# The 47-point products of four sequences, from float32 to one float32r product that carries a rest, with a sum made in DRAM

## Chip, core and metric

The kernel runs on one core of a Trainium2 chip. A core has five engines that run their own queues in order and meet through semaphores: TensorE (PE, matrix products into PSUM), VectorE (DVE), ScalarE (ACT), GpSimd (POOL) and SyncE (SP). SP issues most transfers; POOL issues some, and those that add to what stands at their destination. The metric is the device time of one execution in microseconds (us); less is better. Before the change it is 2776.86 us (median of three runs, 2776.58 to 2780.26).

## What is computed

```python
# x: (8, 3008, 256)
X = rfft(x, axis=1)                                  # along the sequence
Yr = Xr @ w_r - Xi @ w_i + b_r
Yi = Xr @ w_i + Xi @ w_r + b_i
Y  = sign(Y) * max(abs(Y) - 0.01, 0)                 # real and imaginary part apart
y  = irfft(Yr + 1j * Yi, n=3008, axis=1)
t  = y.reshape(24064, 256)
out = (sigmoid(t @ w_gate) * (t @ w_val)) @ w_out    # 1536 hidden columns
```

The inputs are float32, the weights of the last line float64.

## The kernel before

The transform over 3008 = 47 x 64 points is done in two steps. The step that the change touches is the first, "a": for each of the 64 residues, a 47-point real transform, that is a product with a matrix of 47 rows and 48 columns (24 frequencies, real and imaginary). `fa` holds this matrix twice, once for each of two interleaved halves j of the residues, so that one float32 product of 94 rows, 96 output rows and 512 columns (two residues of 256 channels) does both halves. One step `(b, h)` of sequence b covers eight residues: a load `load_a` of 384 KB into a tile `xf` (L181), two products `pa` (L186), two copies from PSUM back into `xf` (L187) and a store `store_a` into the DRAM array `zd` of that sequence (L197). The copies are ACT's, save for one of two in the first two sequences.

The second step reads `zd` back frequency by frequency (`load_b`, tile `zf`, L239), does a 64-point product (`fwd_b`, tile `pb`, L247), mixes channels (`mix`, `pm`, L282), thresholds, and goes back (`inv_b`, `pi`, L319 to L321, then `inv_a`, `pia`, L351). These products, except L247 and L351, are float32r: a value is split into a rounded part and a rest, and the product is the sum of three.

The eight sequences stand in groups of 1, 1, 2, 2 and 2. The dense part (`ffn1`, products `pg` and `pv` at L410 to L412, and `ffn2`, `po` at L438 to L440) of the first nine chunks of tokens runs unit by unit from `ffn`, 108 units in all, and between these units stands the "side" work: the transforms of the later groups. The last two groups' steps "a" are the lists `a3` and `a4`, 16 steps each. Each side piece has a weight (`1.7` for a step "a"), and a piece is issued when enough weight has come together (`rates`, `acc`). From there on the order on each engine is set by a scheduler that works at build time; the earlier part is written out by hand under `manual_schedule`. After the ninth chunk the rest of the dense part runs alone, to the end.

PSUM has eight banks: three for transforms (tag `fft`, so `pa`, `pb`, `pm`, `pi` and `pia` take turns), three for `pg` and `pv`, two for `po`. A bank is free again when ACT or DVE has read it. The tiles of step "a" come from five buffers of 4 KB a partition with the tag `big`; raw weights and, later, `make_t` (POOL's combining of weights, L535 to L551) take buffers of the same tag.

```python
        def step_a(i):
            if i == 0:
                for k in range(min(PRE, len(aa))):
                    load_a(*aa[k])
            if i + PRE < len(aa):
                load_a(*aa[i + PRE])
            fwd_a(*aa[i])
            store_a(*aa[i])
```

Of the kernel before, what the change touches and what calls it, by code (L numbers as in the profile page):

```python
# [9 lines left out]
F32 = mybir.dt.float32  # L10
F32R = mybir.dt.float32r
# [3 lines left out]
ALU = mybir.AluOpType  # L15
# [4 lines left out]
R2, R1 = 47, 64  # L20
NK2 = 24
NQ = 2 * NK2
# [4 lines left out]
HW = 512  # L27
FFT_BANKS, L1_BANKS, L2_BANKS = 3, 3, 2

NF2K, NR2K, NLD, NST, NBIG, NMF, NME, NVF, NVO, NHH, NSG, NYF = 5, 4, 3, 3, 5, 3, 2, 3, 1, 3, 2, 3  # L30
NCB, NTMP, NHP = 10, 9, 12


# [1 line left out]
PRE = 2  # L35
# [13 lines left out]
def _split(v):  # L49
    hi = _r12(v)  # L50
    lo = _r12(v - hi)
    return hi.astype(np.float32), lo.astype(np.float32)
# [13 lines left out]
def _tables(seq):  # L66
    n2 = np.arange(R2)
    k2 = np.arange(NK2)
    c, s = _cs(n2[:, None] * k2[None, :], R2)
    fa = np.zeros((R2, 2, NK2, 2, 2))  # L70
    fb = np.zeros((NK2, 2, 2, 128))
    for j in range(2):
        fa[:, j, :, 0, j] = c
        fa[:, j, :, 1, j] = -s
        fb[:, 0, j, j:2 * R2:2] = c.T / seq
        fb[:, 1, j, j:2 * R2:2] = -s.T / seq
    fa = fa.reshape(2 * R2, 2 * NQ)
    fb = fb.reshape(2 * NQ, 128).astype(np.float32)
    n1 = np.arange(R1)
    k1 = np.arange(R1)  # L80
    mf = np.zeros((NK2, 128, 128), np.float32)
    mi = np.zeros((NK2, 128, 128), np.float32)
    mis = np.zeros((NK2, 128, 2, 128), np.float32)
    for q in range(NK2):
        k = q + R2 * k1
        c, s = _cs(n1[:, None] * k[None, :], seq)
        flip = np.where(k > seq // 2, -1.0, 1.0)
        m = np.zeros((2, R1, 2, R1))
        m[0, :, 0] = c
        m[1, :, 0] = s  # L90
        m[0, :, 1] = -s * flip
        m[1, :, 1] = c * flip
        w = np.full(R1, 2.0)
        if q == 0:
            w[k > seq // 2] = 0.0
            w[(k == 0) | (2 * k == seq)] = 1.0
        e = np.zeros((2, R1, 2, R1))
        e[0, :, 0] = (w * c).T
        e[1, :, 0] = (-w * flip * s).T
        if q:  # L100
            e[0, :, 1] = (w * s).T
            e[1, :, 1] = (w * flip * c).T
        mf[q] = m.reshape(128, 128)
        mi[q] = e.reshape(128, 128)
        mis[q, :, 0], mis[q, :, 1] = _split(e.reshape(128, 128))
    return {"mf": mf, "mi": mi, "mis": mis, "fa": fa.astype(np.float32), "fb": fb}


@with_exitstack
def tile_fft_mix_ffn(ctx: ExitStack, tc, x, w_r, w_i, b_r, b_i, w_one, w_out, mf, mi, mis, fa, fb, out):  # L110
    nc = tc.nc

    B, D, S = x.shape[0], w_r.shape[0], R1 * R2
    P = 128
    XR = x.shape[2]
    CT = D // P
    NF = w_one.shape[0]
    NP = NK2 // 2
# [18 lines left out]
    cw = fft.enter_context(tc.tile_pool(name="cw", bufs=1))  # L137
    p2 = fft.enter_context(tc.tile_pool(name="p2", bufs=2))
# [4 lines left out]
    def bank(name, tag="fft", bufs=FFT_BANKS):  # L143
        return (psf if tag == "fft" else psl).tile([P, 512], F32, tag=tag, bufs=bufs, name=name)
# [5 lines left out]
        gap("gap_r", 320)  # L150
        return p2.tile([P, 2, D], F32R, tag="r2k", bufs=NR2K, name=name)

    fa_sb = cw.tile([2 * R2, P], F32, name="fa_sb")[:, :2 * NQ]
    nc.scalar.dma_start(fa_sb, fa)

    zd = [tc.dram_tile([NQ, R1, D], F32, name=f"zd{b}") for b in range(B)]
# [4 lines left out]
    xv = x.rearrange("b u p (h c) -> b u p h c", c=D)  # L161
# [3 lines left out]
    held = {}  # L165
# [10 lines left out]
    def big(name):  # L176
        return p2.tile([P, 4, D], F32, tag="big", bufs=NBIG, name=name)

    def load_a(b, h):
        xf = p0.tile([P, 4, D], F32, name="xf0", bufs=R1 // 8) if b == 0 else big("xf")  # L180
        nc.sync.dma_start(xf[:XR], xv[b, h])  # L181
        held["x", b, h] = xf

    def product_a(xi, az, copy):
# [4 lines left out]
    def fwd_a(b, h):  # L189

        xf = held["x", b, h]
        for i in range(2):
            at = slice(2 * i, 2 * i + 2)
            product_a(xf[:2 * R2, at], xf[:2 * NQ, at], nc.vector.tensor_copy if b < 2 and i else nc.scalar.copy)

    def store_a(b, h, queue=nc.sync):
        queue.dma_start(zv[b][:, 4 * h:4 * h + 4], held.pop(("x", b, h))[:2 * NQ])  # L197

    def load_half(b, h):
        xf = r2k("xfh").bitcast(F32)  # L200
        nc.sync.dma_start(xf[:XR], xv[b, h // 2, :, h % 2 * 2:h % 2 * 2 + 2])
        held["xh", b, h] = xf

    def half_a(b, h):
# [246 lines left out]
    def fft_units(bs, ms):  # L451


        aa = [(b, h) for b in bs for h in range(R1 // 8)]
        units = []

        def step_a(i):
            if i == 0:
                for k in range(min(PRE, len(aa))):
                    load_a(*aa[k])  # L460
            if i + PRE < len(aa):
                load_a(*aa[i + PRE])
            fwd_a(*aa[i])
            store_a(*aa[i])

        def loads(q, b):
            if b == bs[0]:
                if q == 0:
                    ms[0, 0] = load_mf(0)
                if q + 1 < NP:  # L470
                    ms[q + 1, 0] = load_mf(q + 1)
                if 0 <= q - 1 < NP and (q - 1, 1) not in ms:
                    ms[q - 1, 1] = load_mi(q - 1, False)
            if q == 0:
                load_b(b, 0)
            if q + 1 < NP:
                load_b(b, q + 1)

        def step(q, b):
            loads(q, b)  # L480
            if q < NP:
                fwd_b(b, q, ms[q, 0], False)
            if 0 <= q - 1 < NP:
                mix(b, q - 1)
            if 0 <= q - 2 < NP:
                inv_b(b, q - 2, ms[q - 2, 1], False)

        first = [(1.7, lambda i=i: step_a(i)) for i in range(len(aa))]
        for q in range(NP + 2):
            wt = 0.9 * (q < NP) + 2.0 * (0 <= q - 1 < NP) + 0.7 * (0 <= q - 2 < NP)  # L490
            units += [(wt, lambda q=q, b=b: step(q, b)) for b in bs]
        return first, units
# [259 lines left out]

    bias_sb = cw.tile([P, 2, D], F32, name="bias_sb")
    bias4 = p0.tile([P, D], F32, name="bias4")
    ebias = cw.tile([P, P], F32, name="ebias")[:, :1]
    fb_sb = const.tile([2 * NQ, P], F32, name="fb_sb")
    w1h = const.tile([P, NF, 2, CT, P], F32R, name="w1h")
    w1l = const.tile([P, NF, 2, CT, P], F32R, name="w1l")
# [182 lines left out]
    p0s.close()  # L941
    p3 = p3s.enter_context(tc.tile_pool(name="p3", bufs=2, side="right", reuse_waits="tile"))
    with tc.manual_schedule():
        for u in own0:
            load_v(u)
        load_part()
        halves(AT_FIRST)
        for f in range(NF):
            ffn[f]()
            if parts:  # L950
                load_part()
            if f in (2, 3):
                tables[f - 2, 1] = load_mi(f - 2, False, later=True)
            if f in (5, 6):
                keep_mi(f - 5, tables[f - 5, 1])
            halves(AT_FIRST + (f + 1) * (len(beside) - AT_FIRST) // NF)
# [44 lines left out]
    for j in range(NF, len(ffn)):  # L1001
        c, f = divmod(j, NF)
# [39 lines left out]
    a, b, c, d = banks[0]  # L1042
# [62 lines left out]
```

## Time and profile before

| what | value |
|---|---|
| median of three runs | 2776.86 us (2776.58 to 2780.26) |
| the profiled execution | 2779.58 us |
| its span in the trace | 2777.7 us |
| TensorE clock granted | 0.999 in the mean |
| instructions in the span | 38257 |
| HBM read, written | 134.17 MB, 104.33 MB |

A row of the groups gives the line of the kernel, the engine, the operation, the tile written and the tiles read, the shape, how often, the busy time and the mean duration, and then the time that the engine idled just ahead of these, with what ended it. A row of the stretches gives for each engine the busy time and number of instructions, then PE's granted clock, the mean busy share of the 16 DMA engines, and their rate. PE products overlap in the pipeline; one instruction of float32 appears as two records. PEld is the loading of weights into PE.

### The profile page before, as it was taken

Reading aid. Unit: us, or ns where it says so; the run is one execution under the profiler, and the core shown is the slowest. Engines: PE = TensorE matmul, PEld = TensorE weight load, DVE = VectorE, ACT = ScalarE, POOL = GpSimd, SP = SyncE. Lnnn points to the kernel's source line nnn. Section 1 sums busy time; section 2 is a strip of 40 time slices with the busy share of each in tenths; the row PEclk is TensorE's granted clock in tenths of the full one; section 3 lists DMA queues with packets and bytes.
Section 4 is the critical chain, followed back from the end, with each engine's and each line's share of the span. In section 5 each row is a group of like instructions: output and inputs, shape, how many; then the busy total and the mean of one; then the engine's idle time right before and its main releaser. Section 6 shows DMA issues by size and latency. Waiting matters only on the chain.

```text
span 2777.7 us, 38257 instructions
## 1 busy us (share of the span) xinstructions
PE 2760.4 (99%) x13896; PEld 2305.2 (83%) x13896; DVE 2080.6 (75%) x3109; ACT 1307.4 (47%) x2276; POOL 709.4 (26%) x638
## 2 busy tenths in 40 slices
PE   9999999999999999999999999999999999999999
PEld 6778888888899988888888888888888888888887
DVE  5778778767787636777777777777777777777776
ACT  4665554555455444444444444444444444444443
POOL 0211010223200001333333343333333333333321
PEclk9999999999999999999999999999999999999999
DMA  9867545665554561000000000000000000000000
GB/s 293 266 214 198 171 139 157 193 190 184 178 156 147 168 196 58 31 16 16 31 31 16 16 31 31 31 11 21 31 31 16 16 31 31 27 4 31 31 16 16
DMA packets 173469, 241.01 MB, mean 87 GB/s; under 512 B 14592, under 2 KB 124896, under 8 KB 173280
## 3 DMA queue, kind: packets, MB, share of 16 engines
q1 hardware_dynamic: 163776, 214.93, 25.0%
q0 software_dynamic: 9408, 23.60, 2.6%
q8 instruction: 110, 1.80, 0.3%
q14 instruction: 79, 0.65, 0.1%
q10 hardware_dynamic: 96, 0.04, 0.0%
HBM read 134.17 MB, written 104.33 MB: 86 GB/s over the span
## 4 chain that ended last, share of the span: by engine, by line
PE 95%; DVE 3%; DMA 1%; ACT 1%; issue 0%; SPq 0%; DVEq 0%; ACTq 0%
PE pd L670 11%; PE pc L670 11%; PE pa L670 11%; PE po L646 7%; PE po L645 7%; PE po L647 7%; PE pb L670 6%; PE pm L282 5%; PE pia L351 4%; PE pa L186 3%; PE pb L247 3%; PE pg L410 2%; PE pg L411 2%; PE pg L412 2%; PE pv L410 2%; PE pv L412 2%
## 5 line engine op out<-in xcount | busy, mean ns | idle before, releaser
L647 PE MATMUL po<-hl,w 128*128 128x512 f32 x912 | 354.8, 389 | 0.0
L645 PE MATMUL po<-hh,w 128*128 128x512 f32 x912 | 354.8, 389 | 0.0
L646 PE MATMUL po<-hh,w 128*128 128x512 f32 x912 | 354.8, 389 | 0.0
L729 POOL TENSOR_TENSOR c<-c,c 128x512 f32<-128x512 f32 x114 | 147.7, 1296 | 801.2 <-DVE c L725 588.1
L670 PE MATMUL pc<-s,w1h 128*128 128x512 f32 x912 | 280.8, 389 | 0.0
L670 PE MATMUL pa<-a,w1h 128*128 128x512 f32 x912 | 280.8, 389 | 0.0
L725 DVE TENSOR_TENSOR c<-u,pc 128x512 f32<-128x512 f32 x228 | 156.5, 687 | 91.5 <-PE pc L670 85.6
L700 DVE TENSOR_TENSOR u<-u,pb 128x512 f32<-128x512 f32 x228 | 155.2, 681 | 90.7 <-PE pb L670 61.1
L617 ACT CAST hh<-v 128x512 fp32r<-128x512 f32 x114 | 70.7, 620 | 306.1 <-DVE v L710 306.1
L645 PEld LDWEIGHTS po<-hh,w 128*128 128x128 f32 x912 | 171.2, 188 | 35.6
L670 PEld LDWEIGHTS pc<-s,w1h 128*128 128x128 f32 x912 | 171.2, 188 | 35.5
L670 PEld LDWEIGHTS pa<-a,w1h 128*128 128x128 f32 x912 | 171.2, 188 | 35.5
L647 PEld LDWEIGHTS po<-hl,w 128*128 128x128 f32 x912 | 171.2, 188 | 35.5
L646 PEld LDWEIGHTS po<-hh,w 128*128 128x128 f32 x912 | 171.2, 188 | 35.5
L621 POOL TENSOR_TENSOR hl<-c,hh 128x512 fp32r<-128x512 f32 x114 | 152.3, 1336 | 186.0 <-ACT hh L617 186.0
L282 PE MATMUL pm<-w_sb,xsh 128*128 128x256 f32 x1008 | 188.5, 286 | 1.6 <-ACT xf L187 1.1
L670 PE MATMUL pc<-s,w1l 128*128 128x512 f32 x456 | 177.4, 389 | 0.0
L670 PE MATMUL pa<-a,w1l 128*128 128x512 f32 x456 | 177.4, 389 | 0.0
L702 DVE TENSOR_TENSOR v<-u,pc 128x512 f32<-128x512 f32 x228 | 156.9, 688 | 24.5 <-DVE u L700 0.9
L731 DVE TENSOR_TENSOR u<-u,pd 128x512 f32<-128x512 f32 x228 | 156.6, 687 | 24.5 <-DVE c L725 0.9
L704 DVE TENSOR_TENSOR v<-v,pd 128x512 f32<-128x512 f32 x228 | 156.7, 687 | 24.0 <-DVE v L702 0.5
L696 ACT COPY u<-pa 128x512 f32<-128x512 f32 x228 | 133.7, 586 | 69.4 <-PE pa L670 69.2
(174 smaller groups left out, 6721.1 us busy)
## 6 DMA issues: line engine op xcount, KB each, us to landing
zf<-zd SPq DMA_DIRECT2D x96, 256.0 KB, 3.6
vf<-vd SPq DMA_DIRECT2D x128, 192.0 KB, 3.0
out_dram<-ot SPq DMA_DIRECT2D x93, 256.0 KB, 2.2
vd<-vz SPq DMA_DIRECT2D x84, 256.0 KB, 2.8
ypair<-yd SPq DMA_DIRECT2D x19, 1024.0 KB, 4.9
yd<-yf SPq DMA_DIRECT2D x103, 188.0 KB, 2.9
xf<-in_x_dram SPq DMA_DIRECT2D x48, 384.0 KB, 4.1
zd<-xf SPq DMA_DIRECT2D x44, 384.0 KB, 3.3
```

Source lines behind the costliest of these rows:

```text
L282: nc.tensor.matmul(o, l, r, start=(i == 0), stop=(i == len(mms) - 1))
L621: sub_(hl, h, hh)
L645: nc.tensor.matmul(o, wh, hh, start=(f == 0), stop=False)
L646: nc.tensor.matmul(o, wl, hh, start=False, stop=False)
L647: nc.tensor.matmul(o, wh, hl, start=False, stop=(f == NF - 1))
L670: nc.tensor.matmul(o, l, r, start=not more and l is wh and r is xh, stop=l is wl, skip_group_check=more)
L700: add(u, u, b)
L702: add(v, u, c)
L704: add(v, v, d)
L725: add(c12, u, c)
L729: nc.gpsimd.tensor_mul(c12, g12, c12)
L731: add(u, u, d)
```

## The change

For the steps of `a3` and `a4` only, the float32 product gives way to a float32r product. For each half j (47 rows, of which 64 are loaded; the 17 others meet rows of zeros in the matrix) the step

- loads 64 rows of x into a tile `aw` (SP, L205),
- writes the rounded x into rows 0 to 63 of a tile `xw` (ACT, L212) and minus the rounded x into rows 64 to 127 (ACT, L211),
- lets a transfer of POOL's queue read the same 64 rows of x again and add them to rows 64 to 127 (L213), which then hold the rest x minus its rounding,
- does two products of 128 rows, 128 output rows and 512 columns with the matrix `fw` (L223): its first 48 columns hold the rounded 47-point matrix for the rounded x and, in the lower rows, for the rest; its columns 64 to 111 hold the matrix's own rest for the rounded x,
- copies 112 rows of each result into `aw` (ACT, L224),
- stores rows 0 to 47 into `zd` (SP, L231) and, once that has landed, adds rows 64 to 111 to the same place (POOL's queue, L232).

So a step has four float32r products in place of two float32 ones, four copies in place of two, four splitting instructions, and two loads, two stores and four adding transfers in place of one load and one store. The `big` buffers grow from five to eight; the room comes from the scratch of POOL's transfers (4096 bytes a partition). The weight of a step falls from 1.7 to 0.95. The rows of x are laid out on the host with the halves one after the other, and padded to 112.

```diff
-NF2K, NR2K, NLD, NST, NBIG, NMF, NME, NVF, NVO, NHH, NSG, NYF = 5, 4, 3, 3, 5, 3, 2, 3, 1, 3, 2, 3
+NF2K, NR2K, NLD, NST, NBIG, NMF, NME, NVF, NVO, NHH, NSG, NYF = 5, 4, 3, 3, 8, 3, 2, 3, 1, 3, 2, 3
...
+    fw = np.zeros((128, 128), np.float32)
+    fw[:R2, :NQ], fw[:R2, 64:64 + NQ] = _split(fa[0, :, :, :, 0].reshape(R2, NQ))
+    fw[64:64 + R2, :NQ] = fw[:R2, :NQ]
...
+    def load_w(b, h):
+        for j in range(2):
+            at = xv[b, h, j * R2:j * R2 + 64]
+            r = p2.tile([P, 4, D], F32R, tag="big", bufs=NBIG, name="xw")
+            t = big('aw')
+            nc.sync.dma_start(t[:64], at)
+            held['w', b, h, j] = r, t
+
+    def split_w(b, h):
+        for j in range(2):
+            r, t = held["w", b, h, j]
+            nc.scalar.mul(r[64:], t[:64], -1.0)
+            nc.scalar.copy(r[:64], t[:64])
+            nc.gpsimd.dma_start(r[64:], xv[b, h, j * R2:j * R2 + 64], accum_op=ALU.add)
+
+    def fwd_w(b, h):
+        for j in range(2):
...
+            for i in range(2):
+                pa = bank("pw")
+                at = slice(2 * i, 2 * i + 2)
+                nc.tensor.matmul(pa, fw_sb, r[:, at], start=True, stop=True)
+                nc.scalar.copy(t[:64 + NQ, at], pa[:64 + NQ].rearrange("p (h c) -> p h c", h=2))
+            held["w", b, h, j] = t
+
+    def store_w(b, h):
+        for j in range(2):
+            t = held.pop(("w", b, h, j))
+            z = zd[b][:, j * R1 // 2 + 4 * h:j * R1 // 2 + 4 * h + 4]
+            nc.sync.dma_start(z, t[:NQ])
+            nc.gpsimd.dma_start(z, t[64:64 + NQ], accum_op=ALU.add)
...
         def step_a(i):
-            if i == 0:
-                for k in range(min(PRE, len(aa))):
-                    load_a(*aa[k])
-            if i + PRE < len(aa):
-                load_a(*aa[i + PRE])
-            fwd_a(*aa[i])
-            store_a(*aa[i])
+            for k in (0, 1) if i == 0 else (i + 1,):
+                if k < len(aa):
+                    load_w(*aa[k])
+                    split_w(*aa[k])
+            fwd_w(*aa[i])
+            store_w(*aa[i])
...
-        first = [(1.7, lambda i=i: step_a(i)) for i in range(len(aa))]
+        first = [(0.95, lambda i=i: step_a(i)) for i in range(len(aa))]
...
+        nc.gpsimd.dma_start(fw_sb, fw)
...
-    nc = _bacc.Bacc("TRN2", target_bir_lowering=False, num_devices=1)
+    nc = _bacc.Bacc("TRN2", target_bir_lowering=False, num_devices=1, dynamic_dma_scratch_size=4096)
...
-    x = given["x"].reshape(b, 2 * R2, R1 // 8, 4 * d).transpose(0, 2, 1, 3)
-    given["x"] = np.ascontiguousarray(np.pad(x, ((0, 0), (0, 0), (0, 2), (0, 0))))
+    x = given["x"].reshape(b, R2, 2, R1 // 8, 4 * d).transpose(0, 3, 2, 1, 4).reshape(b, R1 // 8, 2 * R2, 4 * d)
+    given["x"] = np.ascontiguousarray(np.pad(x, ((0, 0), (0, 0), (0, R2 + 64 - 2 * R2 + 1), (0, 0))))
```

How the scheduler places the new work is seen in three pieces of the built order. The lines of the changed file are 38 higher from L238 on (L410 becomes L448, L319 becomes L357). First PE, in a step of the group `a3`, before: the two float32 products stand together behind the `pi` products of a side unit and ahead of a dense unit's `pg`.

```order
L319 MATMUL pi_4227<-yh_4030,mi_sb_3899 128x256
L320 MATMUL pi_4227<-yl_4031,mi_sb_3899 128x256
L321 MATMUL pi_4227<-yh_4030,mi_sb_3899 128x256
L186 MATMUL pa_4239<-xf_3861,fa_sb_77 96x512
L186 MATMUL pa_4242<-xf_3861,fa_sb_77 96x512
L410 MATMUL pg_4246<-yth_1901,w1h_105 128x512
L411 MATMUL pg_4246<-ytl_1902,w1h_105 128x512
```

PE in a step of the same group, with the change: the four products of the two halves (`xw_4262` and `xw_4265`) are spread among the dense unit's products.

```order
L359 MATMUL pi_4437<-yh_4221,mi_sb_4117 128x256
L223 MATMUL pw_4459<-xw_4262,fw_sb_103 128x512
L448 MATMUL pg_4475<-yth_1902,w1h_105 128x512
L449 MATMUL pg_4475<-ytl_1903,w1h_105 128x512
L223 MATMUL pw_4462<-xw_4262,fw_sb_103 128x512
L450 MATMUL pg_4475<-yth_1902,w1l_106 128x512
L448 MATMUL pg_4475<-yth_1902,w1h_105 128x512
L223 MATMUL pw_4465<-xw_4265,fw_sb_103 128x512
```

The products that stood side by side now alternate with others, each with its own FFT bank.

Second ACT, behind those same four products: the four copies into `aw_4263` and `aw_4266`, one dense unit's sigmoid and cast, one transform unit's copies, and then the split of a later step, whose `xw_4649` lies in the buffer that `aw_4263` has had.

```order
L224 COPY aw_4263<-pw_4462 112x512
L331 CAST yh_4433<-yc_4430 128x512
L224 COPY aw_4266<-pw_4465 112x512
L224 COPY aw_4266<-pw_4468 112x512
L454 ACTIVATE sg_4489<-pg_4475 128x512
L464 CAST hh_4492<-sg_4489 128x512
L298 COPY xsf_4515<-pb_4508 128x2x2x2x64
L302 CAST xsh_4513<-xsf_4515 128x768
L361 COPY vz_4561<-pi_4554 128x512
L211 ACTIVATE xw_4649<-aw_4650 64x1024
L454 ACTIVATE sg_4578<-pg_4564 128x512
```

Before, this place on ACT held two copies L187 and nothing of the split.

Third POOL, whose queue had no transfer of step "a" in this group before. The adding stores of the step above stand ahead of the adding loads of the later one.

```order
L213 DMA xw_4447<-in_x_dram 64x1024
L213 DMA xw_4450<-in_x_dram 64x1024
L232 DMA zd5_86<-aw_4263 48x1024
L232 DMA zd5_86<-aw_4266 48x1024
L213 DMA xw_4649<-in_x_dram 64x1024
```

So the adding load into `xw_4649` is issued behind the adding store out of `aw_4263`.

More of the change, by code (lines that the diff above doesn't have):

```diff
@@ L69, in _tables @@
     c, s = _cs(n2[:, None] * k2[None, :], R2)
-    fa = np.zeros((R2, 2, NK2, 2, 2))
+    fa = np.zeros((2, R2, NK2, 2, 2))
     fb = np.zeros((NK2, 2, 2, 128))
     for j in range(2):
-        fa[:, j, :, 0, j] = c
-        fa[:, j, :, 1, j] = -s
+        fa[j, :, :, 0, j] = c
+        fa[j, :, :, 1, j] = -s
         fb[:, 0, j, j:2 * R2:2] = c.T / seq
         fb[:, 1, j, j:2 * R2:2] = -s.T / seq
+    fw = np.zeros((128, 128), np.float32)
+    fw[:R2, :NQ], fw[:R2, 64:64 + NQ] = _split(fa[0, :, :, :, 0].reshape(R2, NQ))
+    fw[64:64 + R2, :NQ] = fw[:R2, :NQ]
     fa = fa.reshape(2 * R2, 2 * NQ)
@@ L105, in _tables, with tile_fft_mix_ffn @@
         mis[q, :, 0], mis[q, :, 1] = _split(e.reshape(128, 128))
-    return {"mf": mf, "mi": mi, "mis": mis, "fa": fa.astype(np.float32), "fb": fb}
+    return {"mf": mf, "mi": mi, "mis": mis, "fa": fa.astype(np.float32), "fw": fw, "fb": fb}
 @with_exitstack
-def tile_fft_mix_ffn(ctx: ExitStack, tc, x, w_r, w_i, b_r, b_i, w_one, w_out, mf, mi, mis, fa, fb, out):
+def tile_fft_mix_ffn(ctx: ExitStack, tc, x, w_r, w_i, b_r, b_i, w_one, w_out, mf, mi, mis, fa, fw, fb, out):
     nc = tc.nc
@@ L114, in tile_fft_mix_ffn @@
     P = 128
-    XR = x.shape[2]
+    XR = 96
     CT = D // P
@@ L151, in r2k @@
         return p2.tile([P, 2, D], F32R, tag="r2k", bufs=NR2K, name=name)
-    fa_sb = cw.tile([2 * R2, P], F32, name="fa_sb")[:, :2 * NQ]
+    fa_all = cw.tile([P, P], F32, name="fa_sb")
+    fa_sb, ebias = fa_all[:2 * R2, :2 * NQ], fa_all[:, 2 * NQ:2 * NQ + 1]
     nc.scalar.dma_start(fa_sb, fa)
@@ L180, in load_a @@
         xf = p0.tile([P, 4, D], F32, name="xf0", bufs=R1 // 8) if b == 0 else big("xf")
-        nc.sync.dma_start(xf[:XR], xv[b, h])
+        nc.sync.dma_start(xf[:XR], xv[b, h, :XR])
         held["x", b, h] = xf
@@ L194, in fwd_a @@
             product_a(xf[:2 * R2, at], xf[:2 * NQ, at], nc.vector.tensor_copy if b < 2 and i else nc.scalar.copy)
+    def load_w(b, h):
[13 more added lines that the diff above has]
+        for j in range(2):
+            r, t = held["w", b, h, j]
+            if t is None:
+                t = big("aw")
+            for i in range(2):
[10 more added lines that the diff above has]
+            nc.gpsimd.dma_start(z, t[64:64 + NQ], accum_op=ALU.add)
     def store_a(b, h, queue=nc.sync):
@@ L200, in load_half @@
         xf = r2k("xfh").bitcast(F32)
-        nc.sync.dma_start(xf[:XR], xv[b, h // 2, :, h % 2 * 2:h % 2 * 2 + 2])
+        nc.sync.dma_start(xf[:XR], xv[b, h // 2, :XR, h % 2 * 2:h % 2 * 2 + 2])
         held["xh", b, h] = xf
@@ L754, in tile_fft_mix_ffn @@
     bias4 = p0.tile([P, D], F32, name="bias4")
-    ebias = cw.tile([P, P], F32, name="ebias")[:, :1]
+    fw_sb = cw.tile([P, P], F32R, name="fw_sb")
     fb_sb = const.tile([2 * NQ, P], F32, name="fb_sb")
```

## The prediction

> **What bounds the kernel now.** I read the page first: the busy shares, then the chain that ended last.
>
> ```profile
> PE 2760.4 (99%) x13896; PEld 2305.2 (83%) x13896; DVE 2080.6 (75%) x3109; ACT 1307.4 (47%) x2276; POOL 709.4 (26%) x638
> PE 95%; DVE 3%; DMA 1%; ACT 1%; issue 0%; SPq 0%; DVEq 0%; ACTq 0%
> ```
>
> TensorE (PE) is busy 99% of the span and carries 95% of the chain. Time taken from PE is therefore time gained, as long as nothing else becomes late in the same place. So the second view is that place: the stage in which the 32 changed steps stand (their products run from 206.7 to 720.9 us), beside the more crowded stretch ahead of it.
>
> ```profile
> L186 PE MATMUL pa<-xf,fa_sb x128: 590/592/647, 206.7 to 720.9; 94*96 94x512 f32 x128
> core 0: us, PE busy (x) PEld busy (x) DVE busy (x) ACT busy (x) POOL busy (x), PEclk, DMA share, GB/s
> 206.00:721.00 515.00, 511.33 (x3144) 434.44 (x3143) 391.19 (x673) 260.76 (x442) 99.32 (x150) 1.00 0.59 178
> 60.00:200.00 140.00, 137.24 (x688) 102.16 (x687) 103.45 (x180) 87.41 (x158) 28.59 (x49) 1.00 0.81 251
> 70.00:140.00 70.00, 68.12 (x342) 49.63 (x341) 53.28 (x93) 44.55 (x81) 16.79 (x29) 1.00 0.87 265
> ```
>
> In the stage of 515 us PE idles 3.67 us (0.7%), ScalarE (ACT) works 260.8 us (51%), the DMA engines have a share of 0.59, and the clock is full. Between 60 and 200 us, with ACT at 62% and DMA at 0.81, PE idles 2.76 of 140 us (2.0%); between 70 and 140 us, with 64% and 0.87, it idles 1.88 of 70 us (2.7%). These three rows are all that the trace says of how PE's idle time grows with the load of its helpers.
>
> **PE: what goes.** The ends of matmuls are modelled, so a product's price is the distance of starts, not its duration.
>
> ```profile
> 525.27 0.39 PE L438 MATMUL po<-hh,w 128*128 128x512 f32 x1
> 525.50 0.39 PE L439 MATMUL po<-hh,w 128*128 128x512 f32 x1
> ...
> 526.40 0.39 PE L440 MATMUL po<-hl,w 128*128 128x512 f32 x1
> 526.63 1.88 PE L186 MATMUL pa<-xf,fa_sb 94*96 94x512 f32 x4
> 528.35 1.06 PE L247 MATMUL pb<-mf_sb,zf 128*128 128x128 f32 x8
> ```
>
> From 525.27 to 526.63 stand six float32r products of 512 columns: 0.227 us each. From 526.63 to 528.35 stands one old step, two float32 products recorded as four: 1.72 us. A new step has four float32r products: 4 x 0.227 = 0.91 us. Removed: 32 x (1.72 - 0.91) = **26.0 us**. A float32r product also starts later behind a float32 one:
>
> ```profile
> 681.81 1.13 PE L351 MATMUL pia<-fb_sb,vf 96*128 96x94 f32 x8 [0.20 <-DVE yt L284]
> 682.73 0.48 PE L410 MATMUL pg<-yth,w1h 128*128 128x512 f32 x1
> 683.04 1.88 PE L186 MATMUL pa<-xf,fa_sb 94*96 94x512 f32 x4
> ```
>
> The first one behind L351 holds 0.31 us instead of 0.23. Steps that stood among float32r work lose one such change; at most 32 x 0.09 = 2.9 us more. I take nothing and keep 2.9 for the low end. The doubled weight loads (64 more) go beside products: PEld is busy 434 of 515 us.
>
> **ACT: what comes.** Per step two copies of 96 x 512 go; four of 112 x 512 come, and two L211 and two L212 of 64 x 1024.
>
> ```profile
> L264 ACT CAST xsh<-xsf 128x768 fp32r<-128x768 f32 x84 | 70.1, 834 | 88.3 <-PE pm L282 70.9 <-DVE xsf L262 14.1 <-DVE yc L271 3.1
> L426 ACT CAST hh<-sg 128x512 fp32r<-128x512 f32 x105 | 65.1, 620 | 82.1 <-DVE sg L418 81.2
> L187 ACT COPY xf<-pa 96x512 f32<-96x512 f32 x80 | 45.8, 581 | 29.0 <-PE pa L186 28.8
> ```
>
> Between the casts of 512 and 768 columns lie 214 ns for 256, so one of 1024 is estimated at 834 + 214 = 1048 ns. Added: 128 x 1.048 + 64 x 0.581 = 171 us. The stage shrinks on PE to 515 - 26 = 489 us, and ACT then works 432 of these: 88%, against 51%. Nothing of it is on PE's path by itself; PE needs ACT to empty the three FFT banks and, later, the two sigmoid banks. What 88% costs PE no row shows. Lower bound: idle stays at 0.7%, nothing new. Upper bound by a straight line through (51%, 0.7%) and (62%, 2.0%): 0.11 points per point, so 4.8% of 489, 23 us. The nearest row (2.7%, by its DMA share, below) gives 13 us. I take the middle of the two, 18.3 us, which is **+14.6** on the present 3.7.
>
> How full ACT is depends on whether neighbours overlap.
>
> ```profile
> 576.51 0.62 ACT L293 CAST yh<-yc 128x512 fp32r<-128x512 f32 x1 [2.09 <-DVE yc L272]
> 577.03 0.46 ACT L343 CAST yth<-pia 128x376 fp32r<-128x376 f32 x1
> 577.40 0.62 ACT L426 CAST hh<-sg 128x512 fp32r<-128x512 f32 x1
> ```
>
> Here each starts 0.10 us before the one ahead has ended. The Trainium skill, ScalarE: Activation LUTs, section What ACT_TABLE_LOAD costs, says that back-to-back ACTIVATEs overlap by about 93 ns; with all of the some 634 instructions of the new stage overlapping, ACT would stand at 432 - 59 = 373 us, 76%, and the straight line would end at 3.5%, 17 us. The trace agrees where nothing is waited for (0.10 us).
>
> **POOL, SP, DMA.** Four accumulating transfers a step are new on POOL's queue, and one load and one store more on SP's.
>
> ```profile
> L209 POOL DMA_DIRECT2D zd<-azh x32 | 16.9, 532 | 62.9 <-ACT azh L187 62.8
> zf<-zd SPq DMA_DIRECT2D x57, 256.0 KB, 3.6
> zd<-xf SPq DMA_DIRECT2D x32, 384.0 KB, 3.2
> xf<-in_x_dram SPq DMA_DIRECT2D x27, 384.0 KB, 3.7
> mi_sb<-in_mis_dram POOLq DMA_DIRECT2D x10, 256.0 KB, 4.3
> td<-tr POOLq DMA_DIRECT2D x12, 512.0 KB, 4.5
> md<-mi_sb POOLq DMA_DIRECT2D x10, 256.0 KB, 3.0
> L197 SPq DMA_DIRECT2D zd<-xf x32: 304/322/609, 209.3 to 722.1; - x32
> ```
>
> POOL: 128 x 0.53 = 68 us on 99, a third of the stage, hidden beside PE since no product waits for POOL's own arithmetic there. SP: 64 more issues x 0.32 = 20 us in 489. Behind a waiting SP load or store stand the zf loads, which PE needs; they are issued one round ahead, and land in 3.6 us. Bytes: loads 512 plain and 512 accumulating instead of 384 KB, stores 384 as before plus 384 accumulating: 1024 KB more a step, 33.6 MB. At 178 GB/s for a share of 0.59, that is 302 GB/s at full share, so 111 us; with the 0.59 x 515 = 304 us now, 415 of 489, a share of 0.85. That is the load of the row 70 to 140, which is why I lean on it. The smaller scratch on POOL's rings: no row shows the rings filling; between nothing and what a rival below gives a late accumulate. The weight 0.95 for 1.7 only spreads the side work anew over the same units; it adds and removes no instruction, and I price it at nothing, with the same two ends. The load of fw_sb is one transfer of 64 KB ahead of the stage.
>
> **Sum.** The profiled execution took 2779.58 us: 2779.58 - 26.0 + 14.6 = 2768.2. It lies 2.7 us above the median of 2776.86, so the forecast is **2766 us**, 0.4% less.
>
> **Rivals.** *The DMA engines become the bound.* If an accumulate occupies them twice (it reads what it adds to), 896 KB x 32 = 29.4 MB count once more, 97 us: 512 us of transfers in a stage of 489. The stage would end at 512, 3 us less than now: 2774. For it: share 0.81 already goes with latencies above 4 us; against: no row shows the price of an accumulate.
>
> *ACT is held by an accumulate that lands late: slower.* ACT works in order. In 17 of the 32 steps the tile xw that L211 writes takes the place of the aw of an earlier step, and must wait until that one's accumulating store has landed; behind L211 stand the sigmoids and bank copies. Between the last copy into that aw and the L211 the order leaves, priced with the rows above, 4.4 to 6.9 us of ACT work, 5.6 in the mean (the piece shown in the change: 5.0), some 6.4 us of time at 88%. The chain in that time is: store to landing 3.2, POOL's issue 0.53, the accumulate's landing X. ACT waits X - 2.7. It has 1.8 us free a step ((489 - 432) / 32); what exceeds that holds PE, 17 times. With X as md (3.0) or mi_sb (4.3) it waits 0.3 to 1.6 us and PE feels nothing; the 26.0 us are gone when X reaches 2.7 + 1.8 + 26.0 / 17 = **6.0 us**. At X = 7.5: 17 x 3.0 = 51, 25 more than now, 2802; at 9, twice the 4.5 of td: 2827. For it: the share rises, and an accumulate moves more than a plain transfer; against: 4.5 us is the most that a POOL transfer takes in this stage.
>
> The Trainium skill speaks against the change here: DMA: Bandwidth & Descriptors, section Rules for kernel authors, has an accumulating DMA wait for the semaphore of the earlier one on the same bytes, because it reads its destination and writes it later; that is the chain above, two landings one behind the other. The same page of the Trainium skill has a fit (Anatomy of one DMA, 2.0 us plus bytes over 436 GB/s) that would make X an estimated 2.5 us, and this rival void; the rows of 3.0 to 4.5 do not bear that out.
>
> *It does not do what it says:* four products on full rows could cost more than 0.227 each. The neighbours L438 to L440 use all 128 rows and columns and show no such price; I give it nothing.
>
> **Chances.** Faster, PE still the bound, 0.47. Within 0.2%, about what a measurement of this kernel can tell from no change (2771.3 to 2782.4): stalls of 20 to 32 us, 0.14, and the DMA rival, 0.06, together 0.20. Slower, ACT held: 0.33, since X stands between 4.5 for a plain transfer and 6.0 where it decides. Range: below, no new stall and the 2.9, 2776.9 - 28.9 = 2748; above, X = 7.5, 2803, leaving out about 0.15 of the slow cases and little below. Within the likeliest case alone: 2748 to 2771.
>
> **What would show it.** Four L223 products 0.23 us apart, and PE some 26 us less busy: the first term. PE's idle in the stage (about 490 to 515 us long) near 18 us and spread over many small waits for ACT copies: the second. ACT's idle ahead of L211 put down to zd transfers, several us each, and accumulates landing after 6 us or more: the slow rival. zf loads landing late at a DMA share near 1: the DMA rival. The forecast is wrong if PE idles over 32 us there, or if the time changes outside 190 to 720 us.

## The result, and the profile after

The changed kernel takes 2849.64 us (median of 4 runs, 2843.15 to 2857.05) beside 2778.14 us for the kernel before on the same chip: 1.0258 times the time, with an interval of 1.0228 to 1.0287. It is 71 us slower, and the forecast (2766, between 2748 and 2803) was too low. The profiled execution took 2857.05 us.

The page of the changed kernel, its lines of span, busy time, POOL's DMA queue and the chain:

```profile
span 2855.1 us, 38969 instructions
PE 2777.4 (97%) x13896; PEld 2328.5 (82%) x13896; DVE 2082.0 (73%) x3109; ACT 1454.9 (51%) x2468; POOL 810.8 (28%) x767
q0 software_dynamic: 18768, 53.03, 9.1%
PE 81%; DMA 6%; ACT 4%; issue 3%; DVE 3%; POOL 1%; SPq 0%; POOLq 0%; ACTq 0%; DVEq 0%
```

Two things stand in the PE entry and the span ahead of it. The span minus PE's busy time is its idle time: 77.7 us, against 17.3 before (2777.7 - 2760.4). And PE is busy for 2777.4 us, 17 us *more* than before, though it has less to do. The chain has fallen from 95% PE to 81%, and transfers, ACT and issue have come in.

The stage, in the view of stretches (columns as in the prediction):

```profile
206.00:721.00 515.00, 464.70 (x2808) 404.23 (x2808) 341.48 (x605) 356.99 (x557) 145.16 (x195) 0.95 0.86 210
206.00:790.00 584.00, 525.65 (x3166) 456.58 (x3166) 385.72 (x673) 400.79 (x626) 177.20 (x245) 0.94 0.87 211
```

In the stretch of 515 us in which before PE worked 511 us at clock 1.00, it now works 465 us at 0.95. ACT's share over the longer stretch is 69%, not 88%: by the pages ACT has 147.5 us more work (1454.9 against 1307.4) where 171 were forecast, and the stage has become much longer. Its end is seen in the new product's own row (durations minimum, median, maximum in ns, then first and last start):

```profile
L223 PE MATMUL pw<-xw,fw_sb x128: 387/416/796, 208.8 to 784.6; 128*128 128x512 f32 x128
```

The last one starts at 784.6; before, the last step's product started at 720.9, and 26 us less were forecast.

Who waits for what in it, from the view of waits between 206 and 800 us (total us, times, longest):

```profile
POOL xw L213 <- ACT xw L211: 178.4, 42, 13.5
POOL zd L232 <- DMA zd<-aw: 68.9, 13, 10.7
ACT xw L211 <- DMA zd<-aw: 33.2, 14, 6.7
ACT xw L211 <- DMA aw<-in_x_dram: 18.2, 6, 6.2
PE pw L223 <- ACT vz L361: 15.8, 5, 5.6
PE pw L223 <- ACT aw L224: 7.6, 3, 5.7
```

PE is seen waiting for a transfer only once, for 0.2 us. It waits for ACT's copies `vz` and `aw`, which empty the banks of the transforms: 23.4 us ahead of the new products, a part of its idle time in the stage. ACT waits, at the head of its queue, with the split, L211, for transfers. The timeline shows one such place on three engines (start, duration, engine, instruction, and in brackets the idle time ahead of it with what ended it):

```profile
617.15 0.47 PE L223 MATMUL pw<-xw,fw_sb 128*128 128x512 f32 x1 [0.24 <-DVE ys L326]
623.25 0.79 PE L223 MATMUL pw<-xw,fw_sb 128*128 128x512 f32 x1 [5.63 <-ACT vz L361]
623.85 0.63 PE L448 MATMUL pv<-yth,w1h 128*128 128x512 f32 x1
...
614.54 0.83 ACT L302 CAST xsh<-xsf 128x768 fp32r<-128x768 f32 x1 [1.36 <-PE pm L320]
621.54 1.05 ACT L211 ACTIVATE xw<-aw 64x1024 fp32r<-64x1024 f32 x1 [6.17 <-DMA aw<-in_x_dram]
622.62 0.58 ACT L361 COPY vz<-pi 128x512 f32<-128x512 f32 x1
...
615.26 1.12 SPq L205 DMA_DIRECT2D aw<-in_x_dram  x2
```

SP issues the loads of `aw` at 615.26. ACT comes to the split and waits 6.17 us for the landing. The copy `vz` stands behind it with no wait of its own; it starts at 622.62, takes 0.58 us, and the product that it releases by emptying a bank starts at 623.25, after 5.63 us of idle PE.

### The profile page after: what moved, and what is told of

It reads as the page before. It is cut to its first block, busy times and chain, and to the rows that moved or that the text cites. A ratio compares the mean times of both kernels' runs of the same rounds, so it can differ in the third digit from the quotient of the medians.

```text
span 2855.1 us, 38969 instructions
## 1 busy us (share of the span) xinstructions
PE 2777.4 (97%) x13896; PEld 2328.5 (82%) x13896; DVE 2082.0 (73%) x3109; ACT 1454.9 (51%) x2468; POOL 810.8 (28%) x767
## 4 chain that ended last, share of the span: by engine, by line
PE 81%; DMA 6%; ACT 4%; issue 3%; DVE 3%; POOL 1%; SPq 0%; POOLq 0%; ACTq 0%; DVEq 0%
PE pd L707 11%; PE pc L707 11%; PE pa L707 11%; PE po L684 7%; PE po L683 7%; PE po L682 7%; PE pb L707 5%; PE pm L320 4%; PE pia L389 3%; DMA zd<-aw 3%; PE pb L285 2%; DMA aw<-in_x_dram 1%; PE pv L448 1%; PE pv L449 1%; PE pv L450 1%
## 5 line engine op out<-in xcount | busy, mean ns | idle before, releaser
L320 PE MATMUL pm<-w_sb,xsh 128*128 128x256 f32 x1008 | 195.3, 293 | 11.8 <-DVE ytl L382 6.1
L320 PEld LDWEIGHTS pm<-w_sb,xsh 128*128 128x128 f32 x1008 | 159.8, 195 | 14.0 <-DVE ytl L382 6.3
```

The costliest lines, as they stand in the source:

```text
L320: nc.tensor.matmul(o, l, r, start=(i == 0), stop=(i == len(mms) - 1))
```

## Experiments

Eighteen further kernels ran, each beside the kernel before (whose medians lie between 2778.5 and 2780.4 us). In brackets stand the ratio to the kernel before and its 95% interval. Expectations were written ahead of each run. "Two banks" and "four banks" are the transform banks that a step fills.

### First: which transfers cost it?

```diff
-            nc.gpsimd.dma_start(z, t[64:64 + NQ], accum_op=ALU.add)      # e1, e3
-            nc.gpsimd.dma_start(r[64:], xv[...], accum_op=ALU.add)       # e2, e3
-                nc.scalar.copy(t[:64 + NQ, at], pa[...])                 # e4
+                nc.scalar.copy(r[:64 + NQ, at], pa[...])
```

> The changed kernel without the adding stores (L232): the correction rows are copied but not added, so the result lacks them. Theory R (late accumulate: ACT stands in L211 for the buffer that an earlier step's adding store still reads, PE then idles and its granted clock falls): most of the added 72 us goes, 2765 to 2790 us, ACT's idle time ahead of L211 below 10 us, clock in the stage back above 0.98. Rival L (ACT's load of some 88% is enough): nothing changes, 2835 to 2855. Rival X (the adding loads L213 are what PE waits for): 2830 or more.

> The changed kernel without the adding loads (L213): the lower rows hold minus the rounded x. Theory R: the adding stores remain, so 2815 to 2850 us and ACT still idles ahead of L211. Rival X: 2765 to 2790. Rival L: 2835 to 2855.

> The changed kernel without either adding transfer; ACT's and PE's work is as in the change. Theory R and rival X: 2755 to 2775 us, that is the 26 us of PE less what ACT's load costs. Rival L: 2835 or more, since ACT's load is untouched; a value of 2785 to 2815 would put about half on ACT's load.

> The changed kernel with the four result copies written into xw, in rounded form, in place of aw; both stores read xw. All transfers and all work remain. aw is free after the split, and a buffer that an adding store reads is taken again three steps later in place of two. Theory R: the wait ahead of L211 goes, 2770 to 2810 us. Rivals L and X: no change, 2835 to 2855.

Measured: e1 2797.31 (ratio 1.0069, 1.0046 to 1.0092); e2 2835.35 (1.0204, 1.0174 to 1.0234); e3 2790.33 (1.0046, 1.0023 to 1.0069); e4 2834.78 (1.0202, 1.0172 to 1.0232). So the adding stores cost 52 us, the adding loads 14 beside them and 7 alone. e1, e3 and e4 are slower than the ranges of theory R, the late accumulate. In e4, `aw` is free once it is split, so that a buffer comes round one step later; the wait of L211 for stores falls from 33.2 to 19.4 us, and the time by some 15. That is the prediction's slow rival: real, but a smaller part of the 52. The surprise is e3: without any adding transfer the kernel is still slower than before, 37 us above what its products should give. In it PE waits for banks again:

```profile
206.00:790.00 584.00, 558.44 (x3555) 490.65 (x3554) 430.70 (x751) 428.81 (x676) 102.35 (x151) 0.99 0.64 181
```

At a DMA share of 0.64, near the 0.59 of before, PE still idles 25.6 us of the 584 (its last new product starts at 727.9).

### Second: load on ACT, accumulate, or the wait?

e5b takes e3 and splits only the first half of the columns; both products read that half. e8 stores the correction rows plainly into an array of their own; e9 adds them to an array that nothing reads any more, so without a wait for the plain store. e7 is another way to do the change: 94 rows as before, three float32r products summed in one bank, seven large buffers, and no adding transfer.

```diff
-            nc.gpsimd.dma_start(z, t[64:64 + NQ], accum_op=ALU.add)
+            nc.gpsimd.dma_start(ze[...], t[64:64 + NQ])                     # e8
+            nc.gpsimd.dma_start(zd[0][...], t[64:64 + NQ], accum_op=ALU.add) # e9
...
-            nc.scalar.mul(r[64:], t[:64], -1.0)                              # e5b
+            nc.scalar.mul(r[64:, :2], t[:64, :2], -1.0)
...
+        nc.scalar.copy(xh[:2 * R2], xf[:2 * R2])                             # e7
+        nc.gpsimd.tensor_sub(xl[:2 * R2], xf[:2 * R2], xh[:2 * R2])
+            for k, (v, z) in enumerate(((0, xh), (0, xl), (1, xh))):
+                nc.tensor.matmul(pa, fw_sb[:, v], z[:2 * R2, at], start=(k == 0), stop=(k == 2))
```

> Leaves out both accumulating transfers, as e3 did, and the split of half of the columns: both products of a row half read the first 512 columns, so ScalarE has 64 x 1.05 = 67 us less and PE the same products. e3 took 2790 where its products alone would give 2753. Theory A, the missing 37 us are ScalarE's load (copies that empty the banks late): half of them or more come back, 2763 to 2775. Theory B, they are late loads of aw behind SP's waiting transfers, or the products' own price: 2785 to 2793.

> The correction rows are stored plainly by POOL into a DRAM tile of their own, so they are not added to the result; no accumulate, and no wait for the plain store's landing. The number of transfers and the written bytes stay. Chain theory (two landings one behind the other, with POOL's queue held between them, is what the adding stores cost): 2790 to 2812, near e1's 2797. Traffic theory (192 KB more a store, one more issue on POOL): 2830 to 2850, near the changed kernel.

> The correction rows are added by the same accumulating transfer, but into the tile of the first sequence, which has been read by then, so the result lacks them; nothing waits for the plain store. Chain theory: the wait for the plain store is gone, 2795 to 2820. If the accumulate itself is the price (it reads and writes, and its issue holds POOL 0.81 us): 2830 to 2850. Between e8 and e9 lies what accumulating costs over storing.

> Before's loads and stores (one of each a step, both halves in one product of 94 rows), but a step is three float32r products per 512 columns, summed in the bank: rounded weights by rounded input, by its rest, and the weights' rest by rounded input. 6 x 0.227 = 1.36 us a step where 1.72 stood: PE -11.5 us, ScalarE +32 x 1.05 = 34 us, the subtraction on POOL. If the loss of the changed kernel comes from its transfers and the doubled ScalarE work, as I think: 2763 to 2772. If even ScalarE's 34 us or POOL's subtraction hold PE: 2775 to 2790.

Measured: e5b 2787.17 (1.0029, 1.0016 to 1.0041); e8 2810.14 (1.0113, 1.0098 to 1.0128); e9 2831.95 (1.0189, 1.0173 to 1.0206); e7 2793.57 (1.0057, 1.0042 to 1.0072). Theory A fell: 49 us less of ACT's work (1405.1 against 1454.3 by the pages; 67 were expected) give back 3. e8 lies at the upper end of the chain theory's range, e9 in the range of the accumulate as the price, and e7 above both of its ranges. From e1 over e8 and e9 to the changed kernel (2797, 2810, 2832, 2850) the adding store's 52 us part into 13 for one more store, 22 for adding instead of storing, and 18 for the wait behind the plain store; no theory alone. What adding changes is seen in POOL's issue of this transfer (minimum, median, maximum of its duration in ns), in e8:

```profile
L234 POOL DMA_DIRECT2D ze<-aw x64: 512/533/804, 210.6 to 747.6; - x64
```

and in e9:

```profile
L233 POOL DMA_DIRECT2D zd<-aw x64: 767/782/1331, 208.6 to 770.4; - x64
```

and in the landings (KB each, median us from issue). In e8, between 200 and 800 us:

```profile
zf<-zd SPq DMA_DIRECT2D x63, 256.0 KB, 4.5
ze<-aw POOLq DMA_DIRECT2D x64, 192.0 KB, 4.9
```

In e9:

```profile
zf<-zd SPq DMA_DIRECT2D x59, 256.0 KB, 5.6
zd<-aw POOLq DMA_DIRECT2D x64, 192.0 KB, 6.0
```

The add itself lands 1.1 us later than the store, and so does a plain load of `zf` that has nothing to do with it. The add also occupies the DMA engines longer. The rows of POOL's DMA queue on the pages (packets, MB, share of 16 engines' span), in e1, e8 and e9:

```profile
q0 software_dynamic: 14672, 40.45, 6.4%
q0 software_dynamic: 18768, 53.03, 7.8%
q0 software_dynamic: 18768, 53.03, 9.0%
```

Of their spans of 2794.4, 2804.1 and 2829.0 us these are 179, 219 and 255 us. So the 64 plain stores of e8 take 40 us of the engines' time, and the 64 adding stores of e9, with the same bytes, 76: nearly twice as much.

### Third: the products alone, and the due weight

x2 is the kernel before with one edit: four float32r products a step on a constant tile (the step's own product is left out, so that these products wait for no load), nothing else. w1 and w2 exchange the weights 1.7 and 0.95; w7 is e7 with 1.7 for its 1.4.

```diff
+        w = w1h[:, 0].rearrange("p i t n -> p (i t n)")                      # x2
+            for v in range(2):
+                nc.tensor.matmul(pa, w[:2 * R2, :2 * NQ], w[:2 * R2], start=True, stop=True)
...
-        first = [(1.7, lambda i=i: step_a(i)) for i in range(len(aa))]       # w1; the reverse in w2
+        first = [(0.95, lambda i=i: step_a(i)) for i in range(len(aa))]
```

> The kernel before, with one edit: each of its 32 steps issues, per 512 columns, two float32r products of 94 rows that read a constant tile of weights, instead of the float32 product of the loaded input (so the result lacks these products). Loads, copies, stores, order and due times stay. It is the changed kernel's PE time without its split, its transfers and its due times. If PE alone is the bound and the first term (26.0 us) is right: 2750 to 2756. If the shorter steps leave the other engines' chains uncovered: 2762 to 2778.

> The kernel before, with the weight of a step in the merged order 0.95 in place of 1.7, which the prediction priced at nothing. If that holds: 2776 to 2782. If the new spread of the side work costs the 20 to 30 us that e3, e5b and e7 lack in common: 2795 to 2810.

> The changed kernel, with the weight back at 1.7. Weight priced at nothing: 2840 to 2860. If the new spread costs 20 to 30 us: 2815 to 2830.

> e7 (three float32r products, split on ScalarE and POOL) with the weight back at 1.7 instead of 1.4. If the spread is what e7 lacks: 2768 to 2778, at or below the kernel before. If it is POOL's subtraction, which slows VectorE (2129 us busy in place of 2081): 2788 to 2800.

Measured: x2 2758.54 (0.9928, 0.9911 to 0.9945); w1 2780.59 (1.0007, 0.9997 to 1.0016); w2 2846.90 (1.0241, 1.0220 to 1.0263); w7 2799.76 (1.0073, 1.0054 to 1.0093). The weight is nothing, and w7 lies in the range given to POOL's subtraction. The products alone give 20.4 us: between the two ranges, and nearer to the first. The page of x2:

```profile
span 2756.3 us, 38246 instructions
PE 2737.4 (99%) x13896; PEld 2305.9 (84%) x13896; DVE 2084.2 (76%) x3109; ACT 1307.4 (47%) x2276; POOL 709.8 (26%) x638
```

PE's work has shrunk by 23.0 us, and its idle time grown by 1.6 (18.9 for 17.3). So 32 us part e3 from x2.

### Fourth: banks

y1 gives each product of x2 a bank and a copy of its own. y2 takes e3, and y6 the changed kernel, and sums the two halves in one bank (which mixes them) and stores both from one tile. y4 is w7 with its subtraction on DVE.

```diff
+                pa = bank("pa")[:2 * NQ]                                     # y1: inside the loop over v
...
+        t = pair[0][1]                                                       # y2, y6
...
+            pa = bank("pw")
+            for j in range(2):
+                nc.tensor.matmul(pa, fw_sb, pair[j][0][:, at], start=(j == 0), stop=(j == 1))
+            nc.scalar.copy(t[:64 + NQ, at], pa[:64 + NQ].rearrange("p (h c) -> p h c", h=2))
...
-        nc.gpsimd.tensor_sub(xl[:2 * R2], xf[:2 * R2], xh[:2 * R2])          # y4
+        nc.vector.tensor_sub(xl[:2 * R2], xf[:2 * R2], xh[:2 * R2])
```

> x2 (2758.5) with one edit: each of the four products of a step goes into a bank of its own and is copied out by ScalarE (two copies of 96 x 512 more a step, 64 x 0.58 = 37 us of ScalarE), as in the changed kernel; before and x2 have two banks a step. No split, no transfer added. If the four banks, in turn with the FFT's own three, are what e3 lacks: 2775 to 2792. If they are not: 2757 to 2764.

> e3 (2790.3, no adding transfers) with the two row halves summed in one bank, so a step fills two banks and has two copies instead of four (the halves are mixed; both are stored from one tile). If the banks are e3's loss: 2762 to 2775. If it is the loads, the split or their order: 2783 to 2792.

> The changed kernel (2849.6) with the same edit: both halves summed in one bank, two copies a step, all adding transfers kept (the halves are mixed). If the banks cost the same here as in e3, some 15 to 30 us go: 2820 to 2835. If the adding transfers' waits have taken their place: 2840 to 2855.

> w7 (three float32r products, 2799.8) with the subtraction of the rounded input on VectorE instead of POOL. If POOL's subtraction held VectorE (43 us more busy): VectorE has some 32 x 1.3 = 42 us more of its own instead, and the time is 2770 to 2785. If the price is the longer way from load to product or ScalarE's cast: 2792 to 2802.

Measured: y1 2766.30 (0.9956, 0.9939 to 0.9972); y2 2773.79 (0.9984, 0.9974 to 0.9993); y6 2813.49 (1.0124, 1.0107 to 1.0141); y4 2824.89 (1.0164, 1.0149 to 1.0180). y1 lies between its two ranges, y2 in the range of the banks, y6 below both of its own. Two more banks a step, with their two copies, cost 8 us where all else is as before (y1); two fewer gain 17 beside the split (e3 against y2) and 36 beside the adding transfers (the changed kernel against y6). It is not ACT's load alone: by the pages y2 spares ACT 31 us of copies and gains 17, e5b spares 49 and gains 3. That it is the turn of three banks is not shown either, since no run changes the banks and nothing else. In y2 and y6 the second `aw` of a step is also free once it is split, as in e4. In y6 L211 no longer waits for any store of `zd` (33.2 us in the changed kernel), and in y2 its waits for transfers fall from 22.4 to 6.7 us. So 8 us are the banks with their copies; the 17 and the 36 hold the earlier buffers too. The groups of the new products between 206 and 800 us (busy, mean ns, then idle ahead of them with what ended it), in e3:

```profile
L222 PE MATMUL pw<-xw,fw_sb 128*128 128x512 f32 x128 | 52.7, 436 | 14.0 <-ACT vz L359 8.1 <-ACT aw L223 3.3 <-DVE ys L324 2.0
```

and in y2:

```profile
L221 PE MATMUL pw<-xw,fw_sb 128*128 128x512 f32 x128 | 40.3, 415 | 2.2 <-DVE yt L320 0.9 <-ACT vz L359 0.6 <-DVE ys L324 0.6
```

The idle time ahead of them falls from 14.0 to 2.2 us. In the changed kernel it is the largest piece of PE's idle time in the stage:

```profile
L223 PE MATMUL pw<-xw,fw_sb 128*128 128x512 f32 x128 | 54.8, 451 | 35.3 <-ACT vz L361 15.8 <-ACT aw L224 7.6 <-ACT yf L405 6.1
```

y4 missed both of its ranges: it is 25 us slower than w7, though DVE's subtraction takes half of POOL's time. The groups point to a reason. In e7, which is w7 but for the weight, on POOL (the window from 206 to 760 us):

```profile
L202 POOL TENSOR_TENSOR xl<-xf,xh 94x1024 fp32r<-94x1024 f32 x30 | 74.1, 2470 | 248.2 <-DMA zd<-xf 150.2 <-ACT xsh L283 23.9 <-PE pa L212 23.7
```

In y4, on DVE:

```profile
L202 DVE TENSOR_TENSOR xl<-xf,xh 94x1024 fp32r<-94x1024 f32 x30 | 37.0, 1235 | 46.9 <-DMA td<-tr 22.4 <-issue 12.2 <-DMA zd<-xf 6.5
```

The subtraction waits above all for transfers, which must leave its buffer. On POOL 248 us of such idle time hold few others; on DVE, which empties banks and feeds PE, 47 us of it stand ahead of everything behind: PE waits 31.8 us for DVE's `yt` ahead of `pia` in y4, 2.0 us in w7. It is the same pattern as ACT's split at 621.54 above. That this idle time is what makes the 25 us is read from the trace; no run took it away alone.

### Fifth: what is left between x2 and y2

y8 halves y2's split as e5b did e3's. y9 puts the changed kernel's eight buffers and smaller scratch into x2.

```diff
-                nc.tensor.matmul(pa, fw_sb, pair[j][0][:, at], start=(j == 0), stop=(j == 1))   # y8
+                nc.tensor.matmul(pa, fw_sb, pair[j][0][:, :2], start=(j == 0), stop=(j == 1))
...
-NF2K, ..., NBIG, ... = 5, 4, 3, 3, 5, 3, 2, 3, 1, 3, 2, 3                    # y9
+NF2K, ..., NBIG, ... = 5, 4, 3, 3, 8, 3, 2, 3, 1, 3, 2, 3
-    nc = _bacc.Bacc("TRN2", target_bir_lowering=False, num_devices=1)
+    nc = _bacc.Bacc("TRN2", target_bir_lowering=False, num_devices=1, dynamic_dma_scratch_size=4096)
```

> y2 (2773.8: no adding transfers, two banks a step) with half of the columns split, 67 us less of ScalarE, the products reading the first half twice. If ScalarE's load is what y2 lacks against x2's 2758.5: about half of the 15 us come back or more, 2760 to 2767. If it is the two smaller loads and stores and the longer way from load to product: 2770 to 2775.

> x2 (2758.5, the products alone) with eight large buffers instead of five and the scratch of 4096 on POOL's rings. Priced at nothing in the prediction: 2756 to 2761. If they are part of the 15 us: 2764 to 2774.

Measured: y8 2766.22 (0.9950, 0.9935 to 0.9964); y9 2756.00 (0.9917, 0.9899 to 0.9935). Buffers and scratch are nothing where no adding transfer runs. With two banks, half of the split is 8 of the 15 us, so the split does cost there; the 3 us that e5b gained beside four banks are not clear of the noise.

## Why the forecast was wrong, point by point

One way from before to the changed kernel, each rung a run (PE busy and idle from its page, idle being span minus busy; the last column is ACT's wait for transfers ahead of its first split instruction, from the view of waits between 206 and 800 us):

| kernel | median | step | PE busy | PE idle | ACT waits |
|---|---|---|---|---|---|
| before (beside x2) | 2779.0 | | 2760.4 | 17.3 | |
| products alone (x2) | 2758.5 | -20.4 | 2737.4 | 18.9 | |
| + split, smaller plain transfers, products of the input (y2) | 2773.8 | +15.3 | 2744.2 | 29.7 | 6.7 |
| + four banks for two, later free buffer (e3) | 2790.3 | +16.5 | 2752.0 | 40.8 | 22.4 |
| + adding loads (e1) | 2797.3 | +7.0 | 2755.3 | 39.1 | 18.2 |
| + correction rows stored plainly (e8) | 2810.1 | +12.8 | 2757.9 | 46.2 | 29.6 |
| + added instead of stored (e9) | 2832.0 | +21.8 | 2767.8 | 61.2 | 46.1 |
| + wait for the plain store (changed kernel) | 2849.6 | +17.7 | 2777.4 | 77.7 | 54.7 |

A step of this table is uncertain by 5 to 9 us (the ratios' intervals), so the 7 of the adding loads are not clear of it, and the shares hang on the order: y2's edit is 17 here and 36 when it is made last (y6).

The last two columns rise together. On this ladder PE's idle time stays within some 4 us of x2's 18.9 plus ACT's wait; e2, e4, w2 and y6 fit within 5, while e5b and y8, which split half, lie 7 to 10 lower. No run took this wait alone away; e4 comes nearest, with 11 us less of it and 13 us less idle PE. So the wait at the head of ACT's queue is the likely common cause of most rungs, and that is read from the traces.

**The first term, 26.0 us less on PE, held in kind and was a fifth too large.** x2 shows 20.4 in the medians, 23.0 in PE's busy time. The allowance of 2.9 for a change of mode, kept for the low end only, does not show.

**The second term, "I take the middle of the two, 18.3 us, which is +14.6", is the step that failed.** It made PE's new idle time a function of how full ACT is. Measured, PE's idle is 60.4 us above before, not 14.6. It is the form that failed and not only the input: at the measured 69% of ACT the straight line gives 2.7%, 16 of the 584 us, and PE idled 58 of them. The straight line left out two things that the order had shown: a step now takes four of the transform banks where it took two, and the split, which waits for transfers, stands in the queue of the engine that empties those banks. The prediction named the three banks and gave them no price of their own.

**A term was missing: the clock.** The prediction read the granted clock as full and left it so. The profiled execution took 88.9 us more than the sum of 2768.2: 45.8 of these are idle time (60.4 for 14.6) and 43.0 busy time (17.0 more where 26.0 less were forecast). Against x2, the changed kernel's span is 98.8 us longer (2855.1 - 2756.3): 58.8 of it idle (77.7 - 18.9), 40.0 more busy time (2777.4 - 2737.4). The mean granted clock is 0.987 here and 0.999 in x2. An estimate from these: 0.013 x 2855.1 - 0.001 x 2756.3, some 34 us. By it most of the 40.0 is the half rate behind gaps, which the last section shows.

**ACT held by a late accumulate, given 0.33, was there and on the right side, but not at its price.** That the time came out slower is not this term's doing alone. It was to decide at X = 6.0; X is 5.8 in the stage. At this X its formula gives 17 x (5.8 - 2.7 - 1.8) = 22 us, so a time about even with before. ACT's waits of this kind are 33.2 us (14 times), and lengthening the way of a buffer (e4) wins some 15. Most of what the adding stores cost is elsewhere: in the traffic, the adding and POOL's queue held behind a landing (e8, e9). The landings, from the view of DMA between 200 and 800 us of the changed kernel:

```profile
xw<-in_x_dram POOLq DMA_DIRECT2D x60, 256.0 KB, 5.1
zf<-zd SPq DMA_DIRECT2D x56, 256.0 KB, 5.2
zd<-aw SPq DMA_DIRECT2D x64, 192.0 KB, 3.7
zd<-aw POOLq DMA_DIRECT2D x64, 192.0 KB, 5.8
```

The Trainium skill's fit (DMA: Bandwidth & Descriptors, Anatomy of one DMA) made X an estimated 2.5 us. The 5.8 us of the adding store here are more than twice that, and the 4.9 us of e8's plain store about twice.

**"POOL: 128 x 0.53 = 68 us ... hidden" and the zf loads "issued one round ahead".** An adding transfer holds POOL 0.81 us in the median (L213 and L232), not 0.53, POOL is busy 101 us more by the page (810.8 against 709.4), and POOL's queue stands 69 us ahead of L232 for the plain store's landing, with the next adding loads behind it. zf lands in 5.2 us instead of 3.6; PE is not seen waiting for it.

**The DMA share, 0.85 forecast and 0.87 measured, agrees by luck.** The share was forecast for a stage of 489 us with 111 us of added transfers. By the pages the queues' shares come to 28.0% of 2777.7 us before and 34.7% of 2855.1 after: 213 us more. That is close to the count of the DMA rival, 111 + 97, whose condition held: an accumulate occupied the engines nearly twice as long as a store (e8, e9). Its consequence, the engines as the bound, is not seen: PE waits 0.2 us for a transfer, and y6 has a share of 0.91 between 206 and 790 us and is 36 us faster.

**What was right:** the weight, the buffers and the scratch at nothing (w1, w2, y9). y9 has no adding transfers on POOL's rings; in the changed kernel none of their issues holds POOL over 1.31 us, so no full ring is seen. "It does not do what it says" was nearly rightly left at nothing: the L223 at 289.75 is followed by the next product after 0.23 us, but others without a wait after 0.34.

None of the versions that compute the corrected result beats the kernel before: the nearest are e7 (2793.6) and w7 (2799.8). The runs below 2779 leave the adding transfers or the step's own product out. What remains open is how the 22 us for adding divide between POOL's longer issue and the later landings, and what the 15 us between x2 and y2 are beside the split: the second loads and stores, and products that wait for their input, were not tried alone. Open, too, is what banks cost apart from copies and buffers.

## What to carry to other kernels

An instruction that waits for a transfer costs by its queue, not by its length. At the head of the queue of the engine that empties PSUM banks, its wait can become PE's, as at 621.54; on an engine that empties none it costs by what stands behind it, as POOL's wait for the plain store did with its 18 us. Before a PE term is booked as a gain, count the banks that the new step takes from a shared ring, since each must be emptied once more; here two banks and their copies were 8 us alone. And when PE's idle time is forecast, add the slow stretch that can stand behind a gap of some us to the gap itself.

## What the runs showed of the hardware that was not expected

Behind 13 of its 16 gaps of 1.4 us or more between 206 and 800 us of the changed kernel, PE runs at half its rate, for some 3 to 4 us in the two cases shown. From the timeline of PE, around a gap of 1.40 us, with one of 0.21 us ahead of it (start, duration):

```profile
290.22 0.39 PE L449 MATMUL pg<-ytl,w1h 128*128 128x512 f32 x1
290.82 0.47 PE L223 MATMUL pw<-xw,fw_sb 128*128 128x512 f32 x1 [0.21 <-DVE ys L326]
292.69 0.55 PE L223 MATMUL pw<-xw,fw_sb 128*128 128x512 f32 x1 [1.40 <-ACT vz L361]
293.04 0.63 PE L450 MATMUL pg<-yth,w1l 128*128 128x512 f32 x1
293.47 0.63 PE L448 MATMUL pg<-yth,w1h 128*128 128x512 f32 x1
...
295.60 0.63 PE L449 MATMUL pv<-ytl,w1h 128*128 128x512 f32 x1
296.03 0.58 PE L450 MATMUL pv<-yth,w1l 128*128 128x512 f32 x1
296.44 0.39 PE L448 MATMUL pv<-yth,w1h 128*128 128x512 f32 x1
296.67 0.40 PE L449 MATMUL pv<-ytl,w1h 128*128 128x512 f32 x1
```

From 293.04 to 296.03 the products start 0.43 us apart, from 296.44 on 0.23. Behind the gap of 5.63 us shown above, the stretches give the granted clock itself:

```profile
623.20:625.00 1.80, 1.75 (x4) 1.46 (x5) 0.00 (x0) 1.78 (x3) 0.49 (x1) 0.50 0.50 135
625.00:627.00 2.00, 2.00 (x6) 1.51 (x6) 0.69 (x1) 1.98 (x4) 0.80 (x1) 0.50 0.91 180
627.00:629.00 2.00, 2.00 (x10) 1.61 (x9) 0.00 (x0) 1.25 (x3) 0.00 (x0) 0.87 1.17 241
629.00:631.00 2.00, 2.00 (x18) 1.92 (x16) 0.00 (x0) 1.08 (x3) 0.00 (x0) 1.00 0.51 80
```

0.50, 0.50, 0.87 and 1.00: full speed is back some 4 us after the restart. But the length of a gap alone does not decide. Behind a gap of 2.81 us, twice as long as the first, the products of 512 columns start 0.24 and 0.23 us apart at once:

```profile
226.26 0.39 PE L357 MATMUL pi<-yh,mi_sb 128*128 128x256 f32 x1 [2.81 <-ACT yh L331]
226.48 0.40 PE L448 MATMUL pv<-yth,w1h 128*128 128x512 f32 x1
226.72 0.40 PE L449 MATMUL pv<-ytl,w1h 128*128 128x512 f32 x1
226.95 0.39 PE L450 MATMUL pv<-yth,w1l 128*128 128x512 f32 x1
```

The granted clock is 1.00 from 226 to 230 us, and also from 267 to 271 us, behind a gap of 2.55 us. What decides is open. The Trainium skill, TensorE: Matmul & The Clock Gate, section HAM oscillation — how this bites in real kernels, states the rule as no PE-idle gaps over some 3.4 us. The trace agrees in the half rate; it differs in the length, since here a gap of 1.40 us was enough, while 2.81 us were not.

An accumulating transfer holds POOL 0.78 us at its issue where the same plain one holds it 0.53 (e9, e8), it takes nearly twice the plain one's time of the DMA engines (76 and 40 us for 64), and 192 KB of it land in 5.8 to 6.0 us.
